# Attention with all PSUM banks, then 768 rows of one expert in fp16 parts, instead of fp32 blocks of four experts between

## The chip, the cores and the metric

One of the eight cores of a Trainium2 chip runs the whole kernel. The metric is the device time of one execution in microseconds, as the median of three runs. The core has five engines, each with an instruction queue of its own that is worked off strictly in order: TensorE (PE in the profile; its weight loads are PEld), VectorE (DVE), ScalarE (ACT), GpSimd (POOL), and SyncE (SP), which here only issues DMAs. TensorE writes to PSUM, which has eight banks of 128 x 512 fp32.

## The reference

Attention over 8 batches, 8 heads, 576 positions and 64 dims, causal with a window of 128 and a linear bias; then a mixture of experts over the 4608 tokens (512 wide), each of which goes to the best 2 of 8 experts (512 to 1024 to 512, with relu) by noisy logits.

```python
scores = scale * np.matmul(q, k.transpose(0, 1, 3, 2))
mask = (rel >= 0) & (rel < window)
scores = np.where(mask, scores + bias[None], -1000000000.0)
attn = softmax(scores)                      # in the reference: max, exp, sum + 1e-09
x = np.matmul(attn, v)                      # then tokens x heads*dims: 4608 x 512
noisy_logits = x @ w_gate + np.log1p(np.exp(x @ w_noise)) * noise
top2 = np.argpartition(-noisy_logits, 2, axis=1)[:, :2]      # top2_w: softmax of the two
for e in range(E):
    for k in range(2):
        mask = top2[:, k] == e
        h = np.maximum(x[mask] @ w1[e], 0.0)
        out[mask] += top2_w[mask, k, None] * (h @ w2[e])
```

## The kernel before

All instructions are written out by one Python program, and their order on each engine is set by a planner (class `Order`). Each piece of work is a strand, a generator that asks for an engine with an estimated duration and a rank; when an engine comes free in the planner's clock, it takes the ready piece of the least rank. Tables such as `STAGE`, `GATE`, `LATE`, `TOP`, `SPLIT` and `SIZES` are ranks and estimated durations, so every number in them moves instructions. On the chip the queues then keep that order, whatever the real durations are.

Attention has 96 units: 32 pairs of heads (`k`), each in three groups of query blocks (`GROUPS`). A unit goes through these steps: `scores` (TensorE, L482 and L475, into one of the pairs of banks in the ring `sb`), `top` (Vector: selects the window, L503 and L498, and adds the bias and takes the row's extreme, L508, from PSUM into `p` and `nm`), `soft` (ACT, exp with sum, L515), `trans` (TensorE, L522, into a bank of `tb`), `evac` (ACT or Vector, to `pT`, L262 or L266), `split` (GpSimd, two selects, L542 and L543), `weigh` (TensorE, L563, into a bank of `ob`), and a copy to `xu`. When four pairs have filled a group of a batch, `rows`, `row_major` and `gate` turn it to tokens (L663, L666), send it to DRAM (`xs`) and form the gate logits (L686, L697, L702, L707).

`route(b)` routes a batch: top 2 of the logits, counts by matmuls with a triangle (L754 to L758), places in expert lists (`base`, `line`), and one-hot matrices `hot` (L790, L796) whose product (L801) is the batch's contribution to the lists in DRAM (`slots`), which GpSimd adds by an indirect DMA (L874). In the kernel before, `route(b)` starts when `route(b - 1)` has been sent.

The FFN takes rows of an expert in blocks of up to 512. `tokens` gathers them by indirect DMA (GpSimd, L1068), `turn_tokens` transposes them (TensorE, L1100), `ups` does the first matrix (eight steps f of 128 hidden columns), `middle` applies relu, `downs` does the second, `result` scales and adds rows to `out` by an indirect DMA (GpSimd, L1254). There are two forms:
- first wave, fp32: 256 rows each of experts 0 to 3, of tokens of the first two batches (`CUTS = (2,)`), in the banks that attention leaves (`hb` is bank 5, results in banks of `tb` and `ob`). Matmuls L1117 and L1171.
- second wave, fp16 parts: each weight and each token is split in a high and a low fp16 part, and three products are summed (L1120, L1175, and L1180 where the result comes out turned). The split needs the largest magnitude of an expert's weights (`wam`, L1000 and L1021; `sized[e]`) and the scales of each token (`fit`, L1081 to L1085). It holds the other 960 rows of experts 0 to 3, and 1216 of experts 4 to 7.

What the two waves share is set in these lines:

```python
hb = bank[5]
sb, tb, ob, yb = Ring([bank[0:2]]), Ring([*bank[2:4], bank[7]]), Ring([bank[4], bank[6]]), Ring([])
BLOCKS = (((256, 512), (768, 448)), ((0, 512), (512, 384), (896, 320)))   # (start, rows): experts 0-3, 4-7
```

`banks` gives the score banks to the FFN when all of attention is done, and `second_wave` releases attention's SBUF tiles and makes ten sets of weight tiles when attention and all routing are done. The weights of expert e > 0 are sized once expert e - 1 has begun.

## Time and profile before

| | us |
|---|---|
| median of three runs | 1191.54 (1190.29 to 1195.24) |
| the profiled execution | 1194.33 |
| its span, first to last instruction | 1192.6 |
| TensorE busy in the span | 1125.3 |
| Vector busy | 716.3 |
| ACT busy | 484.9 |
| GpSimd busy | 311.4 |
| first fp32 FFN matmul | 143.1 |
| last of attention's weighing (L563) starts | 299.7 |
| first fp16 FFN matmul | 393.1 |

The page and the views give microseconds from the span's start. A row of a group has line, engine, operation, output and inputs, shape and count, then busy time, mean nanoseconds of one, and the idle time ahead of it with what ended it. Instructions of one engine overlap a little, so a mean times a count can be more than the busy time. The chain of work that ended last gives, from the end back, what each step waited for; its pieces are steps on the path and so show the real spacing of matmuls.

### The profile page before, as it was taken

The numbers are of one execution on the slowest core, as the hardware profiler recorded it, in microseconds if no ns is written. First come the engines' busy times: TensorE is split into PE (matmuls) and PEld (weight loads), VectorE is DVE, ScalarE is ACT, GpSimd is POOL, SyncE is SP. The second block draws the span as 40 slices with busy tenths as digits, with TensorE's granted clock in tenths as the row PEclk, the third lists the DMA queues.
The fourth block names the chain that finished last, engine by engine and source line by source line (L and its number), as shares of the span: only waits on it lengthen the run. The fifth ranks groups of instructions, "written<-read, shape, count | busy, mean of one in ns | idle before, by whom it ended". The sixth has DMA issues, their size and how long they took to land.

```text
span 1192.6 us, 20135 instructions
## 1 busy us (share of the span) xinstructions
PE 1125.3 (94%) x6940; PEld 648.1 (54%) x6940; DVE 716.3 (60%) x2528; ACT 484.9 (41%) x1309; POOL 311.4 (26%) x472
## 2 busy tenths in 40 slices
PE   7998899999998899999999999999989989999995
PEld 4665566666665445445445455456635654575552
DVE  6899988878766825645745745634743673372310
ACT  5776656655124314334334334233413532262311
POOL 2333433325123202311320330233203220232211
PEclk9999999999999999999999999999999999999998
DMA  9897555443658817626636644633823571342221
GB/s 324 271 340 255 155 179 161 152 145 86 186 148 252 246 42 203 173 58 186 173 74 186 177 84 162 177 63 64 244 83 64 123 231 37 63 117 45 36 27 24
DMA packets 133368, 173.32 MB, mean 145 GB/s; under 512 B 25232, under 2 KB 84880, under 8 KB 133264
## 3 DMA queue, kind: packets, MB, share of 16 engines
q1 hardware_dynamic: 115344, 131.68, 34.9%
q0 software_dynamic: 17920, 40.33, 17.8%
q8 instruction: 56, 0.92, 0.3%
q14 instruction: 48, 0.39, 0.1%
HBM read 130.57 MB, written 41.40 MB: 144 GB/s over the span
## 4 chain that ended last, share of the span: by engine, by line
PE 76%; DVE 10%; DMA 9%; issue 2%; POOL 1%; SPq 1%; ACT 1%; POOLq 0%; another core or an unknown queue 0%; DVEq 0%; ACTq 0%
PE bank L1120 26%; PE bank L1175 18%; PE bank L1180 9%; DMA mraw<-in_w_dram 5%; PE bank L563 4%; PE bank L1171 4%; PE bank L1117 3%; PE bank L482 3%; PE bank L1100 2%; DVE wam L1021 2%; PE bank L522 2%; DVE p L508 1%; PE bank L663 1%; DMA raw<-in_w_dram 1%; DMA w1a<-in_w_dram 1%
## 5 line engine op out<-in xcount | busy, mean ns | idle before, releaser
L1161 DVE SCALAR_TENSOR_TENSOR bhl<-bank,bhh 128x512 f16<-128x512 f32 (+3 forms) x160 | 97.3, 608 | 289.9 <-ACT bhh L1142 282.4
L1254 POOL DMA_INDIRECT out_dram<-yo,ix x72 | 113.0, 1570 | 573.6 <-ACT yo L262 468.5
L1120 PE MATMUL bank<-bxh,w1hb 128*128 128x512 f16 (+3 forms) x640 | 222.3, 347 | 0.0
L1120 PE MATMUL bank<-bxl,w1hb 128*128 128x512 f16 (+3 forms) x640 | 222.1, 347 | 0.0
L1120 PE MATMUL bank<-bxh,w1lb 128*128 128x512 f16 (+3 forms) x640 | 222.1, 347 | 0.0
L1142 ACT ACTIVATE bhh<-bank 128x512 f16<-128x512 f32 (+3 forms) x147 | 79.1, 538 | 349.6 <-PE bank L1120 348.0
L1120 PEld LDWEIGHTS <-w1hb 128*128 128x128 f16 x1280 | 124.3, 98 | 105.5 <-issue 2.2
L1175 PE MATMUL bank<-w2hb,bhl 128*128 128x512 f16 (+1 forms) x376 | 144.4, 384 | 1.2 <-DVE bhl L1161 1.2
L1175 PE MATMUL bank<-w2hb,bhh 128*128 128x512 f16 (+1 forms) x376 | 144.8, 385 | 0.5 <-ACT bhh L1142 0.5
L1175 PE MATMUL bank<-w2lb,bhh 128*128 128x512 f16 (+1 forms) x376 | 144.2, 383 | 0.0
L515 ACT ACTIVATE p<-p,nm 128x128 f32<-128x128 f32 x288 | 111.8, 393 | 19.2 <-DVE nm L508 18.6
L1175 PEld LDWEIGHTS <-bhh 128*128 128x128 f16 (+1 forms) x752 | 72.9, 99 | 80.8 <-issue 7.6
L1120 PEld LDWEIGHTS <-w1lb 128*128 128x128 f16 x640 | 62.6, 98 | 55.0
L482 PE MATMUL bank<-qk 64*128 64x256 f32 (+1 forms) x512 | 71.3, 391 | 18.7 <-DVE nm L508 13.1
L542 POOL TENSOR_SCALAR_AFFINE_SELECT pT<-pT 128x256 f32<-128x256 f32 (+2 forms) x96 | 43.9, 457 | 158.7 <-ACT pT L262 97.8
L1068 POOL DMA_INDIRECT xg<-xs_dram,ix x72 | 70.8, 984 | 42.9 <-issue 15.5
L563 PE MATMUL bank<-pT,vraw 128*64 128x128 f32 (+2 forms) x896 | 76.7, 303 | 5.0 <-POOL pT L543 3.7
L1021 DVE TENSOR_REDUCE wam<-mraw 128x1 f32<-128x1024 f32 x56 | 67.3, 1211 | 19.7 <-DMA mraw<-in_w_dram 17.7
L262 ACT ACTIVATE bxh<-bank 128x512 f16<-128x512 f32 (+1 forms) x71 | 40.6, 571 | 82.8 <-PE bank L1100 69.8
L1180 PE MATMUL bank<-bhl,w2hb 128*128 128x448 f16 (+1 forms) x224 | 73.8, 330 | 0.0
L1180 PE MATMUL bank<-bhh,w2lb 128*128 128x448 f16 (+1 forms) x224 | 73.8, 330 | 0.0
L1180 PE MATMUL bank<-bhh,w2hb 128*128 128x448 f16 (+1 forms) x224 | 73.8, 329 | 0.0
(208 smaller groups left out, 1818.6 us busy)
## 6 DMA issues: line engine op xcount, KB each, us to landing
raw<-in_w_dram SPq DMA_DIRECT2D x128, 256.0 KB
mraw<-in_w_dram SPq DMA_DIRECT2D x56, 512.0 KB
qk<-in_qk_dram SPq DMA_DIRECT2D x32, 608.0 KB
vraw<-in_v_dram SPq DMA_DIRECT2D x16, 640.0 KB
out_dram<-xg SPq DMA_DIRECT2D x10, 1024.0 KB
w1a<-in_w_dram SPq DMA_DIRECT2D x32, 256.0 KB
w2a<-in_w_dram SPq DMA_DIRECT2D x32, 256.0 KB
xs_dram<-x SPq DMA_DIRECT2D x32, 256.0 KB
```

What stands on the lines that cost most here:

```text
L482: nc.tensor.matmul(s[h][:, o:o + c], qk[half, i * 128:i * 128 + 128], qk[half, QW + k0:QW + k0 + c], start=True, stop=True)
L515: nc.scalar.activation(pv, pv, AF.Exp, bias=nm[:, z, h:h + 1], scale=-1.0, accum_out=den[:, z, 2 * g + h:2 * g + h + 1])
L563: nc.tensor.matmul(o[half, o0:o0 + c], t[:, kb, hh:hh + D], w, start=m == 0, stop=m == len(lst) - 1)
L1021: yield dve(1.13, rank, lambda: nc.vector.tensor_reduce(o, t, axis=AX.X, op=OP.max, apply_absolute_value=True))
L1068: yield pool(1.04, rank, lambda: nc.gpsimd.indirect_dma_start(out=xg[0:r], out_offset=None, in_=xs[0:blk.rows], in_offset=bass.IndirectOff ...
L1120: nc.tensor.matmul(t[:, 0:blk.n], wp[:, c], x[:, c, 0:blk.n], start=c == 0 and z == 0, stop=c == 3 and z == 2)
L1142: nc.scalar.activation(o, i, AF.Relu)
L1161: yield dve(0.07 + c * 0.00104, rank - MIDDLE, lambda: nc.vector.scalar_tensor_tensor(hl[:, 0:c], t[:, 0:c], 0.0, hh[:, 0:c], op0=OP.max, ...
L1171: nc.tensor.matmul(blk.y[j][0:r], blk.h[f][1][0][:, cs], w[1], start=f == 0, stop=f == 7)
L1175: nc.tensor.matmul(blk.y[j][0:r], h[:, cs], wp, start=f == 0 and m == 0, stop=f == 7 and m == 2)
L1180: nc.tensor.matmul(blk.y[c][:, 0:blk.n], wp[:, c * 128:c * 128 + 128], h[:, 0:blk.n], start=f == 0 and m == 0, stop=f == 7 and m == 2)
L1254: ins = nc.gpsimd.indirect_dma_start(out=out, out_offset=bass.IndirectOffsetOnAxis(ap=blk.ix[0:r, j:j + 1], axis=0), in_=t[0:r], in_offset ...
```

## The change

- Attention gets all eight banks: two pairs of score banks in place of one, two banks each for `tb` and `ob`. The counts of `route` go to a bank of `tb`. No FFN stands between.
- The fp32 wave is gone. `first` is now 768 rows of expert 0, of tokens of the first six batches (`CUT = 6`), as two blocks of 384 in fp16 parts; they stand behind attention and ahead of the other blocks, whose rows are now 448 of expert 0 and 1216 of each other expert. All blocks share one set of rings.
- Expert 0's weights are sized and split during attention into eight sets (`early_sizes`, for experts 0 and 1); the low parts of expert 0's weights are made by GpSimd in two instructions each, others by Vector as before. Ten more sets are added behind attention, as before, so there are 18.
- `route(b)` waits for batch b - 2 in place of b - 1, and has two sets of tiles; only the running counts (`based`) go from batch to batch. For all but the last batch GpSimd builds the one-hot matrices, in 20 instructions (ten of 128 x 80, ten of 128 x 64); Vector did so in eleven.
- The addition to `den` goes from Vector to GpSimd.
- The reads for the maxima of experts 2 to 7 are of 512 KB in one run, where a partition's 4 KB lay 16 KB apart.
- The planner's numbers are others throughout.

```diff
-CUTS = (2,)
-FIRST = (256,)
-NF = 4
+CUT, NF = 6, 1
+FIRST = ((0, 384), (384, 384))
...
-BLOCKS = (((256, 512), (768, 448)), ((0, 512), (512, 384), (896, 320)))
+BLOCKS = (((768, 448),), ((0, 512), (512, 384), (896, 320)))
...
-SIZES = (62.8, 977.3)
-EARLY = 1
+SIZES = (65.9, 147.7, 901.7)
+EARLY = 2
...
-    hb = bank[5]
-    rp = hb[:, 464:512].rearrange("p (i e) -> p i e", i=6)
-    hbr, own = Ring([hb]), Ring([hb])
-    sb, tb, ob, yb = Ring([bank[0:2]]), Ring([*bank[2:4], bank[7]]), Ring([bank[4], bank[6]]), Ring([])
+    sb, tb, ob = Ring([bank[0:2], bank[2:4]]), Ring([bank[7], bank[6]]), Ring([bank[4], bank[5]])
+    hbr, yb = Ring([]), Ring([])
...
-            nc.vector.tensor_scalar(den[0:nr, 0:nz], den[0:nr, 0:nz], 1e-9, None, op0=OP.add)
-            nc.vector.reciprocal(den[0:nr, 0:nz], den[0:nr, 0:nz])
+            nc.gpsimd.tensor_scalar(den[0:nr, 0:nz], den[0:nr, 0:nz], 1e-9, None, op0=OP.add)
+        yield pool(0.4 if nz == 1 else 0.2, rank, sums)
+        yield dve(0.2, rank, lambda: nc.vector.reciprocal(den[0:nr, 0:nz], den[0:nr, 0:nz]))
...
     def route(b):
         yield gates[b]
-        if b:
-            yield routed[b - 1]
+        if b > 1:
+            yield routed[b - 2]
+        y_, u, l, tp, idx, ef, oh, both_, d, gg, rk, oh2, lo_, si, gd, listed, *hot = route_sets[b % 2]
+        on, G = (dve, nc.vector) if b == B - 1 else (pool, nc.gpsimd)
...
-            V.tensor_tensor(hot[0], ef.rearrange("p i k -> p (i k)")[:, :, None].to_broadcast(shape),
-                            steps_[:, None, :].to_broadcast(shape), op=OP.is_equal)
+            if b == B - 1:
...
+            for i in range(NQ):
+                for k in range(2):
+                    G.tensor_scalar(hot[0][:, 2 * i + k], steps_, ef[:, i, k:k + 1], None, op0=OP.is_equal)
...
-                V.tensor_scalar(hot[1][:, 2 * i + k], steps_[:, 0:LINE], d[:, i, k:k + 1], numbers[:, i:i + 1],
+                G.tensor_scalar(hot[1][:, 2 * i + k], steps_[:, 0:LINE], d[:, i, k:k + 1], numbers[:, i:i + 1],
                                 op0=OP.is_equal, op1=OP.mult)
...
+        if b:
+            yield based[b - 1]
         yield from chain(taken, 0.0)
-        put(own, hb)
+        put(tb, a)
+        if b + 1 < B:
+            yield from chain(onward, 0.0)
+        mark(based[b])
...
+    def early_sizes():
+        yield biased[NP - 1]
+        for e in range(EARLY):
+            done = Event(16)
+            for f in range(8):
+                for z, (rg, src) in enumerate(((raw1, w1), (raw2, w2))):
+                    t = yield (rg, SIZES[e])
...
+            yield done
+            yield from powers_of_weights(e, SIZES[e])
...
-                    spawn(largest(rg, t, rank, wam[:, e % 2, z, q:q + 1], dram(src, e * DM * F + q * 1024, [[4096, 128], [1, 1024]]),
-                                  done))
+                    spawn(largest(rg, t, t, 1.13, rank, wam[:, e % 2, z, q:q + 1],
+                                  dram(src, e * DM * F + q * 131072, [[1024, 128], [1, 1024]]), done))
...
-        yield dve(0.6, rank, lambda: nc.vector.scalar_tensor_tensor(lo, t, sc, hi, op0=OP.mult, op1=OP.subtract))
+        def rest_of_weight():
+            nc.gpsimd.tensor_scalar(t, t, sc, None, op0=OP.mult)
+            nc.gpsimd.tensor_tensor(lo, t, hi, op=OP.subtract)
+        if e == 0:
+            yield pool(1.9, rank, rest_of_weight)
+        else:
+            yield dve(0.66, rank, lambda: nc.vector.scalar_tensor_tensor(lo, t, sc, hi, op0=OP.mult, op1=OP.subtract))
...
     def banks():
         yield attended
-        for t in sb.free.pop():
+        scores_ = [t for two in (sb.free.pop(), sb.free.pop()) for t in two]
+        for t in scores_[:3]:
             put(hbr, t)
-        t = yield (ob, 0)
-        put(yb, t)
+        put(yb, scores_[3])
+        for _ in range(2):
+            t = yield (ob, 0)
+            put(yb, t)
```

The order on the engines shows what moves. In the rows below, a name is followed by the number of its buffer (bank_66 to bank_73 are the eight banks, bank_66 and bank_67 the first pair), and x2 or x4 stands for so many instructions alike. First TensorE in the middle of attention, before: the scores of a unit (L482) take the only pair, bank_66 and bank_67, and between them and the next unit's scores stand transposes (L522), weighing (L563) and gate logits (L686).

```order
L482 MATMUL bank_66<-qk_79 128x128
L482 MATMUL bank_67<-qk_79 128x128
L482 MATMUL bank_66<-qk_79 128x256
L482 MATMUL bank_67<-qk_79 128x256
L697 MATMUL bank_69<-ident,gt_116 128x128 x2
L522 MATMUL bank_73<-ident,p_87 128x128
L563 MATMUL bank_72<-pT_94,vraw_82 64x256 x2
L563 MATMUL bank_72<-pT_94,vraw_82 64x128 x4
L686 MATMUL bank_73<-xu_98,wgn 32x256 x4
L482 MATMUL bank_66<-qk_79 128x256
L482 MATMUL bank_67<-qk_79 128x256
```

And now, at a like place (L479 and L472 are the scores, L560 the weighing):

```order
L472 MATMUL bank_68<-qk_81 128x192
L479 MATMUL bank_66<-qk_78 128x128
L479 MATMUL bank_67<-qk_78 128x128
L479 MATMUL bank_66<-qk_78 128x256
L479 MATMUL bank_67<-qk_78 128x256
L560 MATMUL bank_71<-pT_94,vraw_84 64x64 x4
L479 MATMUL bank_68<-qk_78 128x256
L479 MATMUL bank_69<-qk_78 128x256
```

The scores of three units stand nearly in a row, on two pairs of banks. Over the whole of attention TensorE has done the scores of 2.3 pairs of heads (as a mean) more than it has weighed, where it was 1.3.

Next GpSimd's queue in attention, before: selects alone (L542, L543), and a batch's lists going out (L874).

```order
L542 AFFINE_SELECT pT_95<-pT_95 128x128
L543 AFFINE_SELECT pT_95<-pT_95 128x128
L542 AFFINE_SELECT pT_96<-pT_96 128x2x128
L543 AFFINE_SELECT pT_96<-pT_96 128x2x128
L873 MEMSET pad 1x1
L874 DMA slots_dram<-listed,line_of_152 704x64
```

Now (L1045, L1046 the low part of a weight, L788, L793 the one-hot matrices, L632 the addition to den, L539, L540 the selects):

```order
L1045 TENSOR_SCALAR raw_123<-raw_123,wsc 128x512
L1046 TENSOR_TENSOR w2la_221<-raw_123,w2ha_220 128x512
L788 TENSOR_SCALAR hot_175<-steps,ef_164 128x80 x10
L632 TENSOR_SCALAR den_108<-den_108 128x16
L793 TENSOR_SCALAR hot_176<-steps,d_167,numbers 128x64 x2
L632 TENSOR_SCALAR den_109<-den_109 128x16
L793 TENSOR_SCALAR hot_176<-steps,d_167,numbers 128x64 x2
L539 AFFINE_SELECT pT_96<-pT_96 128x128
```

A unit's selects now stand behind eighteen other instructions.

Last, the end of attention on GpSimd now (L539 and L540 the selects of the last units, L1062 the gathers of the first rows of expert 0):

```order
L540 AFFINE_SELECT pT_94<-pT_94 128x2x128
L539 AFFINE_SELECT pT_95<-pT_95 128x4x128
L540 AFFINE_SELECT pT_95<-pT_95 128x4x128
L539 AFFINE_SELECT pT_96<-pT_96 128x128
L540 AFFINE_SELECT pT_96<-pT_96 128x128
L632 TENSOR_SCALAR den_103<-den_103 128x16
L632 TENSOR_SCALAR den_104<-den_104 128x16
L631 COPY den_105<-den_105 64x4
L632 TENSOR_SCALAR den_105<-den_105 64x8
L1062 DMA xg_124<-xs_dram,cl 128x520
L1062 DMA xg_125<-xs_dram,cl 128x520
L1062 DMA xg_126<-xs_dram,cl 128x520
```

The first rows are gathered behind the last select of attention (the lists of batch 5, which they need, go out five units earlier); before, the gathers of the first wave stood among the selects, halfway through attention.

More of the change, by code (lines that the diff above doesn't have):

```diff
@@ L321, in attention_moe @@
     tmp = const.tile([128, 2, E], F32, name="tmp")
-    line_of = [const.tile([E * SPAN, 1], I32, name=f"line_of{z}") for z in range(2)]
+    line_of = [const.tile([E * SPAN, 1], I32, name=f"line_of{z}") for z in range(3)]
     tops = const.tile([2, 1], F32, name="tops")
@@ L584, in unit @@
         s = yield (sb, r0)
-        yield pe((0.95, 1.2, 0.36)[gr], r0, lambda: scores(k, blocks, s), mode="rows" if nz == 2 else "full")
+        yield pe((0.77, 0.98, 0.325)[gr], r0, lambda: scores(k, blocks, s), mode="rows" if nz == 2 else "full")
         left[k] -= 1
@@ L939, in attention_moe @@
     back = keep.tile([128, E], F32, name="back")
-    seen = {(e, f): Event(2) for e in range(EARLY) for f in range(8)}
     sized = [Event() for _ in range(E)]
@@ L1042, in powers_of_weights @@
         mark(sized[e])
-    def all_powers():
-        for e in range(EARLY):
-            for f in range(8):
-                yield seen[e, f]
-            yield from powers_of_weights(e, ranks1[8 * e + 7] + SIZES[0])
     def scaled_weight(t, r, hi, lo, ev, rank, src, e, z, f):
@@ L1091, in turn_tokens @@
         yield order.now + 2.3
-        if blk in second:
-            yield from fit(blk, j, r, xg, rank)
+        yield from fit(blk, j, r, xg, rank)
         a = yield (tb, rank)
@@ L1115, in mm1 @@
         for c in cc:
-            if blk not in second:
-                nc.tensor.matmul(t[:, 0:blk.n], w[0][:, c], blk.xh[:, c, 0:blk.n], start=c == 0, stop=c == 3)
-                continue
             for z, (wp, x) in enumerate(((w[0], blk.xh), (w[0], blk.xl), (w[1], blk.xh))):
@@ L1169, in mm2 @@
         cs = slice(j * 128, j * 128 + r)
-        if blk not in second:
-            nc.tensor.matmul(blk.y[j][0:r], blk.h[f][1][0][:, cs], w[1], start=f == 0, stop=f == 7)
-            return
         hh, hl = blk.h[f][1]
@@ L1246, in result @@
         yield emptied
-        yield blk.back if blk in second else blk.weighed
+        yield blk.back
         t = yield (yor, rank)
@@ L1302, in second_wave @@
         for z in range(4):
-            put(fitr, more.tile([128, 3], F32, name=f"fit{z}"))
-        for z in range(4):
             put(ixr, more.tile([128, 4], I32, name=f"ix{z}"))
@@ L1308, in second_wave @@
         put(yb, t)
-        second.extend(Block(e, s0, c, NPAD, rings2) for e in range(E) for s0, c in BLOCKS[e >= NF])
-        for blk, after_ in zip(second, second[1:] + [None]):
-            blk.last = after_ is None or after_.e > blk.e
-            blk.flip = blk.last and after_ is not None
         for z in range(4):
-            put(ytr, more.tile([128, BLOCKS[0][1][1]], F32, name=f"yt{z}"))
-        steps = [(blk, f) for blk in second for f in range(8)]
-        ranks = [1000 + s for s in range(len(steps))]
-        spawn(ups(1, steps, ranks))
-        spawn(downs(1, steps, [r + 0.5 for r in ranks]))
+            put(ytr, more.tile([128, 448], F32, name=f"yt{z}"))
         spawn(second_tokens())
@@ L1403, in second_tokens @@
             yield from tokens(blk, 1000 + 8 * q - 7 if q else FFN1 - SOON)
+    second.extend(Block(e, s0, c, NPAD, rings) for e in range(E) for s0, c in BLOCKS[e >= NF])
+    for blk, after_ in zip(second, second[1:] + [None]):
+        blk.last = after_ is None or after_.e > blk.e
+        blk.flip = blk.last and after_ is not None
+    steps = [(blk, f) for blk in first + second for f in range(8)]
+    ranks = ranks1 + [1000 + s for s in range(8 * len(second))]
     nc.gpsimd.memset(ones, 1.0)
@@ L1416, in attention_moe @@
     order.at(1.9, lambda: order.dispatch("ACT"))
-    def last_weights():
-        yield named[0, NF - 1, 7]
-        yield from weights(1, lambda e, f: 1000 + step_of(e) + f - 4)
-    steps1 = [(blk, f) for blk in first for f in range(8)]
-    for strand in (loads(), masks(), all_values(), set_ups(), first_wave(), first_tokens(), banks(), second_wave(),
-                   weights(0, lambda e, f: ranks1[8 * e + f] - WEIGHTS), last_weights(), all_powers(),
-                   ups(0, steps1, ranks1), downs(0, steps1, [r + 0.3 for r in ranks1])):
+    for strand in (loads(), masks(), all_values(), set_ups(), first_tokens(), banks(), second_wave(), early_sizes(), weights(),
+                   ups([(*s, r) for s, r in zip(steps, ranks)]), downs([(*s, r + 0.4) for s, r in zip(steps, ranks)])):
         spawn(strand)
```

305 lines of the change are left out of this document (131 added, 174 removed).

## The prediction

> **What bounds the kernel now.** I read the page's busy line first, then a table by stage, then the softmax's progress in the same stages, then the waits inside attention.
>
> ```profile
> PE 1125.3 (94%) x6940; PEld 648.1 (54%) x6940; DVE 716.3 (60%) x2528; ACT 484.9 (41%) x1309; POOL 311.4 (26%) x472
> ```
> ```profile
> 0.00:30.00 30.00, 21.06 (x126) 13.89 (x126) 20.43 (x91) 17.66 (x68) 8.32 (x35) 1.00 1.01 324
> 30.00:143.00 113.00, 99.49 (x968) 68.62 (x969) 105.26 (x559) 74.67 (x325) 44.09 (x89) 1.00 0.80 267
> 143.00:290.00 147.00, 141.43 (x1192) 94.06 (x1191) 120.91 (x621) 85.71 (x371) 51.47 (x104) 1.00 0.48 144
> 290.00:323.00 33.00, 32.85 (x252) 20.92 (x251) 25.83 (x116) 8.41 (x31) 6.79 (x13) 1.00 0.52 153
> 323.00:393.00 70.00, 65.67 (x291) 43.53 (x290) 45.18 (x180) 24.23 (x50) 17.69 (x21) 0.98 0.74 209
> 393.00:480.00 87.00, 83.30 (x420) 41.32 (x418) 47.59 (x110) 30.32 (x52) 17.66 (x20) 1.00 0.55 149
> 480.00:1150.00 670.00, 652.18 (x3544) 351.58 (x3543) 347.70 (x855) 237.71 (x406) 155.98 (x180) 0.99 0.47 117
> ```
> Columns: stage, its length, busy us of PE, PEld, DVE, ACT, POOL, then granted clock, DMA share, GB/s. TensorE is the bound almost everywhere, but not in 30 to 143, where attention runs without FFN: there PE has 99.49/113 = 88% and Vector 105.26/113 = 93%. From 143, with fp32 FFN between, PE has 96% and Vector falls to 82%. From 393 the fp16 FFN holds PE at 96 to 97%.
>
> ```profile
> 0.00:30.00 30.00, 9.17 (x44) 1.00 1.01 324
> 30.00:143.00 113.00, 51.19 (x244) 1.00 0.80 267
> 143.00:290.00 147.00, 58.41 (x283) 1.00 0.48 144
> ```
> These are the softmax line's pieces on ACT (576 in all): 2.16 per us alone, 1.93 beside FFN. So alone attention is limited by Vector, and little faster than in company.
>
> ```profile
> PEld bank L482 <- DVE nm L508: 10.8, 17, 1.3
> PE bank L482 <- DVE nm L508: 6.7, 11, 1.0
> DVE bank L503 <- PE bank L482: 1.5, 3, 0.7
> ```
> In 30 to 143 TensorE's scores wait for Vector's top of the unit before (one pair of score banks), and Vector sometimes for the scores.
>
> **The change, step 1: the matmuls.**
>
> ```profile
> 341.75 1.73 PE bank L1117 x8
> 340.03 1.72 PE bank L1171 x4
> 426.83 2.59 PE bank L1175 x12
> 429.42 2.59 PE bank L1120 x12
> 1062.42 3.26 PE bank L1180 x24
> 412.95 0.44 PE bank L1100 x4
> ```
> From the chain: one fp32 step (256 rows, one f) is 1.73 + 1.72 = 3.45 us; 32 of them are 110.4 us, inside and just behind attention. An fp16 step of 512 rows is 2.59 + 2.59 = 5.18, so 10.12 ns a row (3.26 for 24 matmuls of 320 rows is the same rate). The 1024 rows cost 1024 x 8 x 10.12 ns = 82.9 us in fp16 parts: 27.5 us of PE work less, but all 82.9 now stand behind attention. Token tiles turned stay 80, but eight more lie in the fp16 part; three results fewer are turned back: (8 - 3) x 0.44 = 2.2 us.
>
> So with S the start of fp16 FFN (393 before), the span is 1192.6 - (393 - S) + 82.9 + 2.2 - idle saved later. It breaks even near S = 310. All hangs on S.
>
> **Step 2: Vector's work up to the last top.** By 290, where the tops end, Vector was busy 20.43 + 105.26 + 120.91 = 246.6 us.
>
> ```profile
> L796 DVE TENSOR_SCALAR hot<-steps,d,numbers 128x64 f16<-128x64 f16 x61 | 17.6, 346 | 0.0
> L790 DVE TENSOR_TENSOR hot<-ef,steps 128x800 f16<-128x800 f32 x7 | 7.2, 1033 | 0.0
> L266 DVE COPY pT<-bank 128x512 f32<-128x512 f32 x21 | 14.5, 689 | 5.7 <-PE bank L522 3.1 <-PE bank L475 2.3 <-issue 0.3
> L1000 DVE TENSOR_REDUCE wam<-w1a 128x1 f32<-128x512 f32 x8 | 5.4, 680 | 2.3 <-DMA w1a<-in_w_dram 2.3
> L635 DVE TENSOR_SCALAR den<-den 128x16 f32<-128x16 f32 x16 | 2.8, 177 | 0.0
> ```
> Off Vector: the hot matrices of five batches, 5 x (1.03 + 10 x 17.6/61) = 19.6; additions to den, about 5; evictions and scalings of the fp32 FFN, about 5 (from 290 us of the same list); some seven pT and seven xu copies that the order now gives ACT, about 8. Onto Vector: maxima of a second expert, 16 x 0.68 = 10.9; some dozen high parts of expert 0's weights, about 5.5; one more batch routed before the last top, about 8; small casts, 3. Sum -10, of which the overlap of neighbouring instructions takes a fifth: -8, so 239 us.
>
> GpSimd gets the hot matrices, den and 16 pairs of low parts.
>
> ```profile
> L542 POOL TENSOR_SCALAR_AFFINE_SELECT pT<-pT 128x512 f32<-128x512 f32 x32 | 21.5, 671 | 42.8 <-ACT pT L262 34.4 <-DVE pT L266 7.2 <-DVE d L827 1.0
> L542 POOL TENSOR_SCALAR_AFFINE_SELECT pT<-pT 128x128 f32<-128x128 f32 x32 | 9.4, 293 | 19.8 <-ACT pT L262 18.8 <-DVE pT L266 1.1
> L378 POOL IOTA steps<- 128x80 f16 x1 | 0.2, 209 | 0.0
> ```
> No tensor_scalar runs on POOL here. Nearest are the 128x80 iota (0.21) and the 128x128 select (0.29); the upper end is a 128x512 select (0.67). I take 0.25, the width being 64 to 80. 120 such by the last top are 30 us (25 to 80); the weight pairs 16 x (0.67 + about 1.0) = 27. To 290 the queue was busy 8.32 + 44.09 + 51.47 = 103.9 us by the table, and the same selects stay; with these 57 some 161 of 260 us, 62%. That is no bound by itself; but the queue is in order, the splits stand behind it, and TensorE's weighing behind the splits. Cover: scores now run 2.3 pairs ahead of the weighing in TensorE's order, against 1.3.
>
> ```profile
> L796 DVE TENSOR_SCALAR hot<-steps,d,numbers 128x64 f16<-128x64 f16 x20 | 4.4, 312 | 0.0
> ```
> This is L796 in 330 to 352, with GpSimd quiet: 0.22 us each, against 0.29 in attention. So Vector's instructions that touch only SBUF lose some 0.07 to GpSimd's neighbours. With GpSimd's share going from 103.9/290 = 36% to 62%, but the 80 longest of them gone, I add 3: 242 us. The Trainium skill (SBUF — State Buffer, § Who interferes with whom) says more: a GpSimd instruction and a Vector one that needs the shared port pair exclude each other for the whole instruction. The trace agrees in kind; by full blocking the last top would come some 30 us later, which is the fourth rival.
>
> With double score banks I take Vector at 96% (93% is the row's own value, 100% the other end): T = 30 + (242 - 20.4)/0.96 = 261 (252 to 268).
>
> ```profile
> L1117 PE MATMUL bank<-axh,w1a 128*128 128x256 f32 x119 | 33.7, 393 | 0.0
> L1171 PE MATMUL bank<-w2a,ahh 128*128 128x512 f32 x56 | 28.2, 608 | 0.0
> ```
> These are the FFN groups of 143 to 323. Their durations overlap, so I take the chain's spacing, 1.73/8 and 1.72/4: 119 x 0.216 + 56 x 0.43 = 50. TensorE's own attention work is then the four stages' 294.8 - 50 - 1 (token turns) = 244 us, of which about 236 lie before the last top: 90%. The row had 88%, so it fits, but with little room.
>
> **Step 3: from the last top to the first FFN matmul.** The gathers of the 768 rows stand on POOL behind the last select.
>
> ```profile
> 122.03 1.44 POOL L874 DMA_INDIRECT slots_dram<-listed,line_of  x1 [1.47 <-DVE bank L498]
> 127.81 1.29 SPq L910 DMA_DIRECT2D list<-slots_dram  x2
> 131.89 1.02 POOL L1068 DMA_INDIRECT xg<-xs_dram,cl  x1 [0.70 <-DVE cl L895]
> 143.10 0.60 PE L1117 MATMUL bank<-axh,w1a 128*128 128x256 f32 x2
> ```
> The old cut: scatter 122.03, gather 131.89, first matmul 143.10, that is 9.9 and 11.2 us. The scatter of batch 5 now stands five of 96 units (5 x 261/96 = 13.6 us) ahead of the last select, so the list is there; the gather comes at about T + 6 (softmax, transpose, eviction, split, then the clipped numbers on Vector). Behind it 11.2, plus the fit that first-wave tokens did not have: three tiles of about 1.3 on Vector and 0.7 on ACT, some 4. S = T + 21 = 282 (T + 12 if half is hidden, T + 30 if tokens queue). TensorE has only the last turns for these 20 us, some 8: it idles about 10.
>
> ```profile
> 321.18 0.25 PE bank L686 x8
> 359.22 1.00 POOL L1068 DMA_INDIRECT xg<-xs_dram,ix  x1 [6.05 <-PE bank L1171]
> ```
> The 448 remaining rows of expert 0 need the last two routings. Before, from the last gate logits (321) to the first gather (359) took 38 us; with 15 behind it that is 53, and the FFN of 768 rows covers 768 x 8 x 10.12 ns = 62: hidden.
>
> **Step 4: later idle.** 393 to 480 has 87 - 83.3 = 3.7 us idle, 480 to 1150 has 17.8.
>
> ```profile
> PE bank L459 <- DVE wmx L1029: 5.9, 2, 3.0
> DVE wam L1021 <- DMA mraw<-in_w_dram: 17.7, 14, 2.3
> ```
> It comes at the change of experts: Vector waits in order for maxima of the next expert's weights. One expert more is sized early (-3.7). Contiguous reads and 18 weight sets for 10 may take from 0 to 17.8 of the others; I take 2, since the reduce stays behind the load.
>
> **Sum:** 1192.6 - 111 + 82.9 + 2.2 - 6 = 1160.7. The profiled run was 1194.33, 1.7 above its span and 2.8 above the median 1191.54; so 1160.7 + 1.7 - 2.8 = 1160 as a median.
>
> **Rivals.**
> First, attention becomes TensorE's: both engines full (T = 252), half the transition hidden (S = 264), 15 us of later idle gone: 1192.6 - 129 + 85.1 - 15 - 1 = 1133. For it: double score banks. Against: 244 us of TensorE in 252.
> Second, the start of expert 0 is late: tokens queue behind routing on Vector, S = 300: 1192.6 - 93 + 85.1 - 4 - 1 = 1180. For it: gathers behind the last select. Against: the old cut's 11.2 us.
> Third, slower: TensorE stands, in order, before each batch's list matmuls until GpSimd has built that batch's 20 pieces. At 0.25 they take 5 us, at the 128x512 select's 0.67 13.4, some 8.4 more; six batches make 50 us, S = 332, 1192.6 - 61 + 85.1 - 4 - 1 = 1212. It decides from 5 us a batch (S = 312). Against: ops of 64 to 80 columns.
> Fourth, no change: if each added GpSimd instruction (120 hot, 32 for weights, 32 for den) held up Vector for half its length: 15 + 14 + 2 = 31 us, S = 313, 1193. Against: tops read PSUM, and only routing and weights would be hit.
>
> **Chances.** Likeliest, 1147 to 1174, 0.50; first rival 0.17; second, with all of 1174 to 1185, 0.14; fourth 0.09; third 0.10. About 0.5% (6 us) is what a measurement tells from no change. So faster 0.81, same 0.09, slower 0.10. The range that leaves no more than 2 in 10 out: 1135 to 1190; half of it is S, the rest later idle.
>
> **What would show it.** In the changed profile: the last top near 261 with Vector at 95% or more from 30 on; first fp16 matmul near 282 with about 10 us of idle TensorE ahead; softmax pieces at 2.3 to 2.5 per us; hot pieces on POOL near 0.25; no wait of TensorE over 5 us before the 448 rows; 5.18 us for a 512-row step as now. Wrong if Vector stays below 85% in attention, with TensorE waiting for splits or hot matrices, or if FFN starts after 310.

## The result, and the profile after

The change made the kernel slower: 1207.11 us (median of four runs, 1203.02 to 1208.70) against 1192.53 for the kernel before beside it (1190.29 to 1195.24), ratio 1.0116, 95% interval 1.0081 to 1.0151: a small loss, but clear of the spread. The forecast was 1160. The profiled run took 1203.02 with a span of 1201.1, which is 40.4 us more than the 1160.7 of the sum.

The same stages of the changed kernel (columns as before: window, length, busy us of PE, PEld, DVE, ACT, POOL, granted clock, DMA share, GB/s):

```profile
0.00:30.00 30.00, 23.50 (x183) 16.73 (x184) 22.95 (x128) 22.94 (x98) 10.78 (x41) 1.00 0.86 310
30.00:143.00 113.00, 98.00 (x931) 67.35 (x930) 95.97 (x490) 75.06 (x324) 80.91 (x147) 0.94 0.79 271
143.00:290.00 147.00, 125.83 (x1195) 85.00 (x1193) 120.85 (x642) 91.05 (x382) 117.41 (x224) 0.92 0.51 164
290.00:323.00 33.00, 23.20 (x158) 13.33 (x156) 24.52 (x123) 7.04 (x17) 7.49 (x12) 0.74 0.22 62
480.00:1150.00 670.00, 658.31 (x3776) 373.50 (x3775) 334.81 (x855) 230.36 (x395) 161.40 (x186) 0.99 0.44 106
```

Vector should have been at 96% from 30 on. It is at 95.97/113 = 85% and 120.85/147 = 82%. TensorE is no fuller (87 and 86%), and its granted clock, 1.00 in every attention stage before, is 0.94 and 0.92. The engine that has changed is POOL: 10.78 + 80.91 + 117.41 = 209.1 us up to 290, against 103.9 before and 161 in the prediction.

Cutting attention where routing begins, at 100 us, shows when that happened. First softmax's pieces (ACT busy, clock, DMA share, GB/s), then all engines in the same windows:

```profile
30.00:100.00 70.00, 34.30 (x166) 1.00 0.86 295
100.00:140.00 40.00, 13.21 (x64) 0.83 0.69 232
140.00:262.00 122.00, 48.11 (x232) 0.93 0.59 194
```
```profile
30.00:100.00 70.00, 65.77 (x659) 45.51 (x659) 65.42 (x333) 53.10 (x231) 39.14 (x78) 1.00 0.86 295
100.00:140.00 40.00, 29.23 (x242) 19.55 (x240) 27.69 (x143) 20.27 (x86) 38.93 (x67) 0.83 0.69 232
140.00:262.00 122.00, 105.08 (x1011) 71.27 (x1011) 105.41 (x565) 79.57 (x333) 97.69 (x180) 0.93 0.59 194
```

Up to 100 us attention runs as forecast: 166/70 = 2.37 pieces per us, TensorE and Vector both at 93 to 94%. From 100 to 140 it falls to 1.60, Vector to 69%, and POOL stands at 38.93/40 = 97%. What POOL runs there, from its groups by shape up to 300 us (count, busy us, mean ns of one, idle before):

```profile
L793 POOL TENSOR_SCALAR hot<-steps,d,numbers 128x64 f16<-128x64 f16 x60 | 34.5, 595 | 0.5
L788 POOL TENSOR_SCALAR hot<-steps,ef 128x80 f16<-128x80 f16 x60 | 27.8, 481 | 0.5 <-DVE ef L764 0.3
L1045 POOL TENSOR_SCALAR raw<-raw,wsc 128x512 f32<-128x512 f32 x16 | 25.5, 1592 | 4.4 <-DVE lo L761 2.8 <-DVE w1ha L263 1.1 <-DVE both L823 0.4
L1046 POOL TENSOR_TENSOR w1la<-raw,w1ha 128x512 f16<-128x512 f32 x8 | 9.4, 1170 | 0.7
```

In what follows the ten pieces of L788 (128x80) are a batch's line pieces, the ten of L793 (128x64) its place pieces. They take 0.48 and 0.60 us each, not 0.25, so a batch's twenty take 10.8 us; a low weight part takes 1.59 + 1.17 = 2.76, not 1.67. How that reaches TensorE is seen in the first batch routed (timeline of the changed kernel; start, us, engine, line, and in brackets how long the engine had been idle and for whom):

```profile
118.37 4.59 POOL L788 TENSOR_SCALAR hot<-steps,ef 128x80 f16<-128x80 f16 x10
...
122.95 2.24 POOL L793 TENSOR_SCALAR hot<-steps,d,numbers 128x64 f16<-128x64 f16 x4
123.58 0.21 PE L798 MATMUL bank<-hot,hot 128*80 128x64 f16 x1 [4.94 <-POOL hot L793]
...
124.46 0.22 DVE L803 COPY listed<-bank 80x64 f32<-80x64 f32 x1 [4.86 <-PE bank L798]
125.14 0.42 POOL L539 TENSOR_SCALAR_AFFINE_SELECT pT<-pT 128x256 f32<-128x256 f32 x1
```

TensorE stands before a list matmul for 4.94 us, Vector behind it for 4.86, and the next split (L539) comes only after ten line pieces and four place pieces. The ten line pieces are not this batch's: its own had run from 103.65, and eight of its place pieces by 118.4. They are the second batch's, which the order puts ahead of the first batch's last two place pieces; that can happen because `route(b)` no longer waits for batch b - 1. Over attention the waits are (us, times, longest), of PE and then of DVE, both from 100 to 290:

```profile
PE bank L798 <- POOL hot L793: 9.6, 7, 4.9
PE bank L560 <- POOL pT L540: 8.9, 7, 3.2
```
```profile
DVE den L635 <- POOL den L632: 7.4, 5, 2.6
DVE listed L805 <- PE bank L798: 7.3, 4, 3.1
DVE listed L803 <- PE bank L798: 4.9, 1, 4.9
```

All five wait for POOL, directly or by one step. The end of it, from the timeline: the last top, the first gather, the first FFN matmul.

```profile
282.76 0.29 DVE L505 CUSTOM_DVE_ANT_0 p<-bank,bias 128x128 f32<-128x128 f32 x1
290.68 1.09 POOL L1062 DMA_INDIRECT xg<-xs_dram,cl  x1 [1.78 <-DVE l L815]
307.99 0.52 PE L1107 MATMUL bank<-xh,w1ha 128*128 128x384 f16 x1
```

So T = 283 in place of 261 and S = 308 in place of 282. What lies behind S, after and before:

```profile
308.00:1150.00 842.00, 818.35 (x4618) 456.10 (x4617) 438.81 (x1167) 291.85 (x500) 210.88 (x251) 0.99 0.45 111
```
```profile
393.00:1142.00 749.00, 727.48 (x3917) 388.49 (x3915) 393.68 (x960) 265.75 (x453) 173.63 (x200) 0.99 0.48 121
```

TensorE has 90.9 us more work (85.1 were forecast) and 23.7 us idle in place of 21.5 (15.5 were forecast). Counted to the end, 893.1 us follow S; 878.7 were forecast.

### The profile page after: what moved, and what is told of

Its sections match the earlier page's. It is cut to its first block, busy times and chain, and to the rows that moved or that the text cites. A ratio compares the mean times of both kernels' runs of the same rounds, so it can differ in the third digit from the quotient of the medians.

```text
span 1201.1 us, 20775 instructions
## 1 busy us (share of the span) xinstructions
PE 1111.9 (93%) x7192; PEld 649.4 (54%) x7192; DVE 696.6 (58%) x2491; ACT 493.9 (41%) x1327; POOL 432.4 (36%) x676
## 4 chain that ended last, share of the span: by engine, by line
PE 60%; DMA 5%; DVE 5%; issue 1%; ACT 0%; POOL 0%; another core or an unknown queue 0%; POOLq 0%; DVEq 0%; ACTq 0%
PE bank L1107 28%; PE bank L1151 21%; PE bank L1156 8%; DMA mraw<-in_w_dram 4%; PE bank L1093 2%; DVE wam L1014 2%; DMA raw<-in_w_dram 1%; DVE xl L1100 0%; DMA xg<-xs_dram,ix 0%; PE bank L1209 0%; DVE hl L1142 0%; DMA xg<-xs_dram,cl 0%; DVE yo L263 0%; DVE fit L1079 0%; POOL out_dram L1228 0%
## 5 line engine op out<-in xcount | busy, mean ns | idle before, releaser
L1142 DVE SCALAR_TENSOR_TENSOR hl<-bank,hh 128x384 f16<-128x384 f32 (+3 forms) x192 | 110.8, 578 | 296.1 <-ACT hh L1127 295.7
L1151 PEld LDWEIGHTS <-hh 128*128 128x128 f16 (+1 forms) x928 | 89.4, 98 | 96.6 <-issue 5.8
L1107 PE MATMUL bank<-xh,w1hb 128*128 128x320 f16 (+2 forms) x384 | 129.9, 338 | 0.0
L1107 PE MATMUL bank<-xl,w1hb 128*128 128x320 f16 (+2 forms) x384 | 129.9, 338 | 0.0
L1107 PE MATMUL bank<-xh,w1lb 128*128 128x320 f16 (+2 forms) x384 | 129.8, 338 | 0.0
L1107 PE MATMUL bank<-xl,w1ha 128*128 128x384 f16 (+3 forms) x384 | 129.7, 338 | 0.0
L1107 PE MATMUL bank<-xh,w1ha 128*128 128x384 f16 (+3 forms) x384 | 129.7, 338 | 0.0
L1107 PE MATMUL bank<-xh,w1la 128*128 128x384 f16 (+3 forms) x384 | 129.7, 338 | 0.0
L1151 PE MATMUL bank<-w2ha,hl 128*128 128x512 f16 (+1 forms) x234 | 89.3, 382 | 1.2 <-DVE hl L1142 1.2
L1151 PE MATMUL bank<-w2ha,hh 128*128 128x512 f16 (+1 forms) x234 | 89.4, 382 | 0.0
L560 PE MATMUL bank<-pT,vraw 128*64 128x128 f32 (+2 forms) x896 | 76.4, 306 | 9.6 <-POOL pT L540 9.6
L1062 POOL DMA_INDIRECT xg<-xs_dram,ix x74 | 72.4, 979 | 34.1 <-issue 15.2
L479 PE MATMUL bank<-qk 64*128 64x256 f32 (+1 forms) x512 | 72.4, 404 | 12.8 <-DMA qk<-in_qk_dram 6.5
```

Of the source, the lines that this page charges most:

```text
L479: nc.tensor.matmul(s[h][:, o:o + c], qk[half, i * 128:i * 128 + 128], qk[half, QW + k0:QW + k0 + c], start=True, stop=True)
L560: nc.tensor.matmul(o[half, o0:o0 + c], t[:, kb, hh:hh + D], w, start=m == 0, stop=m == len(lst) - 1)
L1062: yield pool(1.04, rank, lambda: nc.gpsimd.indirect_dma_start(out=xg[0:r], out_offset=None, in_=xs[0:blk.rows], in_offset=bass.IndirectOff ...
L1107: nc.tensor.matmul(t[:, 0:blk.n], wp[:, c], x[:, c, 0:blk.n], start=c == 0 and z == 0, stop=c == 3 and z == 2)
L1142: yield dve(0.07 + c * 0.00104, rank - MIDDLE, lambda: nc.vector.scalar_tensor_tensor(hl[:, 0:c], t[:, 0:c], 0.0, hh[:, 0:c], op0=OP.max, ...
L1151: nc.tensor.matmul(blk.y[j][0:r], h[:, cs], wp, start=f == 0 and m == 0, stop=f == 7 and m == 2)
```

## The experiments

In real_prices and hot_on_vector_planned the planner orders everything anew, and before_hot_on_gpsimd has the order of the kernel before. In all other kernels the planner sees the same prices, so every engine's order is that of the changed kernel, save that the named instructions are issued on another engine or slot. Medians are of 4 to 12 runs. T is the last top and S the first fp16 FFN matmul in the profiled run. The kernels ran on several chips, so they are best compared by the ratios, each to the kernel before on the same chip.

| kernel | median us | ratio (95%) | T | S |
|---|---|---|---|---|
| the changed kernel | 1207.1 | 1.0116 (1.0081 to 1.0151) | 283 | 308.0 |
| hot_on_vector | 1188.8 | 0.9949 (0.9925 to 0.9972) | 270 | 295.3 |
| low_on_vector | 1203.1 | 1.0062 (1.0038 to 1.0087) | 278 | 302.6 |
| hot_low_on_vector | 1192.9 | 0.9969 (0.9951 to 0.9986) | 273 | 298.2 |
| real_prices | 1202.1 | 1.0036 (1.0010 to 1.0062) | 280 | 306.1 |
| half_hot | 1188.5 | 0.9961 (0.9942 to 0.9980) | 268 | 293.0 |
| other_half | 1192.0 | 0.9963 (0.9946 to 0.9979) | 271 | 295.8 |
| half_hot_block | 1195.6 | 1.0024 (0.9996 to 1.0051) | 278 | 303.4 |
| spread_line | 1210.7 | 1.0159 (1.0124 to 1.0193) | 291 | 315.3 |
| hot_on_scalar | 1211.0 | 1.0162 (1.0129 to 1.0196) | 284 | 308.5 |
| hot_on_vector_planned | 1199.3 | 1.0052 (1.0032 to 1.0073) | 289 | 296.0 |
| before_hot_on_gpsimd | 1238.0 | 1.0387 (1.0346 to 1.0429) | | |
| half_hot_warm | 1188.8 | 0.9960 (0.9942 to 0.9979) | 269 | 296.1 |
| half_hot_warm_free | 1188.0 | 0.9946 (0.9922 to 0.9969) | 269 | 294.1 |
| half_hot_warm_long | 1188.3 | 0.9931 (0.9918 to 0.9944) | 271 | 297.2 |

**Which of GpSimd's new work.** First the hot matrices, then the low parts, then both go back to Vector.

```diff
-        on, G = (dve, nc.vector) if b == B - 1 else (pool, nc.gpsimd)
+        on, G = dve if b == B - 1 else pool, nc.vector      # hot_on_vector; line pieces as one wide compare
```
```diff
-            nc.gpsimd.tensor_scalar(t, t, sc, None, op0=OP.mult)
-            nc.gpsimd.tensor_tensor(lo, t, hi, op=OP.subtract)
+            nc.vector.scalar_tensor_tensor(lo, t, sc, hi, op0=OP.mult, op1=OP.subtract)   # low_on_vector
```

> The hot matrices of batches 0 to 6 are built by Vector again (one wide compare and ten narrow ones a batch) at the very places where GpSimd had them; the order of TensorE and of all other work is that of the changed kernel, row for row. Theory A, GpSimd's queue holds attention up once routing begins (at 100 us): GpSimd loses some 62 us up to 283, Vector gains about 24, its idle time takes them; tops end near 270 in place of 283, FFN starts near 295, the time falls by 10 to 15 to about 1194, and TensorE's granted clock is near 1.0 from 100 to 260. Theory B, the two in-order queues of TensorE and Vector wait on each other whatever GpSimd does: Vector's 24 us come on top, tops end at 283 to 300, time 1207 to 1225.

> The 16 low weight parts of expert 0 are made by Vector (one instruction of 0.66 us each) in place of GpSimd's pairs of 1.59 and 1.17; TensorE's order unchanged. Theory A: GpSimd loses 44 us, Vector gains 10.6; tops end near 275, time about 1199. Theory B: tops end at 283 to 294, time 1207 to 1218.

> Both of these moves. GpSimd is then about as busy as before the change (some 100 us up to 283), Vector has 35 us more. Theory A: tops end between 262 and 270 with Vector at 97% or more, FFN starts near 290, time about 1188 to 1192. Theory B: tops end at 285 or later, time 1210 to 1240.

Theory A held, theory B fell: T and S come where A had them, and the time falls by 18 us (20 by the ratios) although Vector gets the work back. The windows of hot_on_vector:

```profile
100.00:140.00 40.00, 33.76 (x303) 22.95 (x300) 38.79 (x195) 24.08 (x103) 25.25 (x36) 0.83 0.76 248
140.00:262.00 122.00, 107.78 (x1031) 72.28 (x1029) 117.55 (x610) 80.52 (x334) 68.14 (x118) 0.94 0.60 195
```

Vector is now at 97 and 96%, as forecast for the change itself, POOL at 63 and 56%. One thing of A did not come: the clock is 0.83 and 0.94, as before the move. The low parts alone give 4 us (6 by the ratios) of the 8 expected, and the two intervals just overlap. Both moves together give no more than the first; Vector is at 97% in both windows by then.

**The load or the order?** The planner charged 4.2 us for a batch's hot pieces, which take 10.8.

```diff
-        yield on(0.98 if b == B - 1 else 2.2, rank, which_line)
+        yield on(0.98 if b == B - 1 else 4.8, rank, which_line)
-            yield on(0.4, rank, lambda: which_place(i))
+            yield on(0.6 if b == B - 1 else 1.2, rank, lambda: which_place(i))
-            yield pool(1.9, rank, rest_of_weight)
+            yield pool(2.75, rank, rest_of_weight)
```

> Only the planner's prices change: ten line pieces 4.8 us in place of 2.2, two place pieces 1.2 for 0.4, a low part 2.75 for 1.9, as measured; engines as in the changed kernel, the order planned anew. Theory A (the load on GpSimd itself): GpSimd still has the same 200 us, gain at most 5, time 1202 to 1210. Theory C (the order: the planner put bursts of cheap-looking pieces ahead of splits): the burst of ten pieces no longer stands before a split or a list matmul that is due, waits of TensorE for hot pieces under 3 us in all, tops end near 270, time about 1194.

1202.1, at theory A's lower end: an order that knows the prices wins 5 us (9.5 by the ratios) of the 47 missed. It does keep TensorE from standing before list matmuls, but TensorE's weighing still waits 9.1 us for splits from 100 to 290, against 8.9. The order counts too, though: hot_on_vector planned anew, with Vector's prices, is 10 us slower than in the inherited order.

> As hot_on_vector, but the planner knows that Vector builds them (0.98 us for the line, 0.6 for a pair of place pieces) and orders everything anew. If the engine's load decides, the time is that of hot_on_vector within 5 us, 1184 to 1194. If the order is what decides, tops end 5 or more earlier, time under 1183.

```diff
-        on, G = (dve, nc.vector) if b == B - 1 else (pool, nc.gpsimd)
+        on, G = dve, nc.vector                              # the planner is told 0.98, and 0.6 for a pair
```

Neither expectation. From 100 to 140 us it is worse than the changed kernel (36 softmax pieces for 64). POOL's timeline there, and PE's waits from 100 to 140:

```profile
116.76 2.42 POOL L1045 TENSOR_SCALAR raw<-raw,wsc 128x512 f32<-128x512 f32 x1 [6.48 <-ACT w1ha L261]
...
131.15 1.47 POOL L877 DMA_INDIRECT slots_dram<-listed,line_of  x1 [3.13 <-DMA slots_dram<-listed,line_of]
```
```profile
PE bank L560 <- POOL pT L540: 5.0, 2, 4.4
PE bank L746 <- DVE x L663: 4.3, 1, 4.3
```

POOL stands 6.48 us before a low weight part, works off three of them, and stands 3.13 before a scatter; no split lies between, and weighing waits 4.4 for the next. It is the same fault as the hot pieces', with other work.

**How much of the hot work is too much.** Two kernels leave half of it on GpSimd: the place pieces (half_hot, 5.8 us a batch) or the line pieces (other_half, 4.8).

```diff
-            if b == B - 1:
+            if True:                                        # half_hot: one wide compare on Vector, all batches
-                G.tensor_scalar(hot[1][:, 2 * i + k], ...
+                V.tensor_scalar(hot[1][:, 2 * i + k], ...   # other_half, alone
```

> Of each batch's twenty hot pieces only the ten for the line go back to Vector, as one wide compare of about 1.05 us; the ten for the place stay with GpSimd. TensorE's order unchanged. Load theory: GpSimd loses 6 x 4.8 = 29 of the 62 us up to the last top, so about half of the 18 us that moving all of them gave: tops end near 276, time 1195 to 1200. If what matters is the single longest burst of ten pieces ahead of a split, nearly all of it comes back: 1189 to 1193. If GpSimd were not the limit: 1207 or more.

> The mirror of half_hot: the ten place pieces of a batch go back to Vector (0.3 us each, at the slots where GpSimd had them), the ten line pieces stay on GpSimd as one block of 4.8 us. TensorE's order unchanged. Sum theory (what counts is a batch's GpSimd time against the 4.2 us that the order leaves for it): nearly nothing is lost, 1187 to 1194, less or equal to half_hot_block (5.8 in one block). Block theory (a block ahead of splits costs 1 to 2 us each time whatever the sum): 1195 to 1201.

Either half gives back what moving all gave, within the intervals: the loss is not proportional to the load. Two more kernels change only where in GpSimd's queue the same pieces lie. half_hot_block issues half_hot's ten place pieces in one block in the first slot; spread_line keeps all twenty on GpSimd, but deals the ten line pieces out over the five later slots.

```diff
-                return                                      # half_hot_block, on half_hot: in which_line's slot
+            for i in range(NQ if b < B - 1 else 0):
+                for k in range(2):
+                    G.tensor_scalar(hot[1][:, 2 * i + k], ...
```
```diff
-                    G.tensor_scalar(hot[0][:, 2 * i + k], ...   # spread_line, on the changed kernel
             for k in range(2):                              # in which_place(i)
+                if b < B - 1: G.tensor_scalar(hot[0][:, 2 * i + k], ...
                 G.tensor_scalar(hot[1][:, 2 * i + k], ...
```

> GpSimd has exactly the pieces of half_hot (ten place pieces a batch, the line compare on Vector), but issued as one block of ten (5.8 us) in the first slot, not as five pairs with room for splits between. TensorE's order unchanged. Burst theory: the loss returns, 1198 to 1207. Load theory: as half_hot, 1185 to 1192.

> All hot pieces stay on GpSimd, the same 62 us of them up to the last top; only the block of ten line pieces (4.8 us without a split between) is dealt out over the five later slots, two line and two place pieces (2.2 us) to a slot. TensorE's order unchanged. Burst theory (what counts is how long a due split or list matmul stands behind GpSimd work that is not due): nearly all of the 18 us comes back, tops end at 268 to 272, time 1187 to 1194. Load theory (62 us more on GpSimd, wherever): nothing comes back, 1203 to 1210.

With half the work the block costs 7 us, in the direction of the burst theory, though 1195.6 lies between the two ranges. TensorE's weighing waits for splits from 100 to 290 in half_hot, then in half_hot_block:

```profile
PE bank L560 <- POOL pT L540: 1.6, 4, 0.6
```
```profile
PE bank L560 <- POOL pT L540: 6.9, 5, 2.8
```

With all of the work on GpSimd, spreading gives nothing back, against the burst theory. Waits of spread_line from 100 to 290, PE and DVE:

```profile
PE bank L798 <- POOL hot L793: 19.7, 15, 5.6
PE bank L560 <- POOL pT L540: 6.8, 4, 6.0
```
```profile
DVE listed L805 <- PE bank L798: 24.0, 5, 5.7
```

The splits now come between (8.9 to 6.8), and the list matmuls wait for it: 9.6 to 19.7, and Vector behind them 24. So both are limits: a batch's pieces have some 4 to 6 us in this order. 4.8 fit even as one block, 5.8 fit if splits may pass, and 10.8 fit in none of the three layouts tried (as planned, spread, and planned with real prices). Why a block of 4.8 costs nothing and one of 5.8 costs 7 us is not shown further; Vector's share of the pieces differs too between those two kernels.

**One part alone, in the kernel before.** The same twenty pieces go to GpSimd, with nothing else changed.

```diff
-                V.tensor_scalar(hot[1][:, 2 * i + k], ...
+                (V if b == B - 1 else nc.gpsimd).tensor_scalar(hot[1][:, 2 * i + k], ...   # line pieces likewise
```

> The kernel before, with only this part of the change: the hot matrices of batches 0 to 6 built by GpSimd in twenty narrow pieces, everything else and the order as before. Load theory with cover: GpSimd is at 36% there, TensorE has fp32 FFN steps to run, batches are routed one after another, so little shows: 1190 to 1200. Rival: a burst of some 10 us ahead of splits and the list matmuls costs its 2 to 3 us a batch wherever it stands: 1205 to 1215.

Both expectations were far too small: 45 us, 6.4 for each of seven batches. POOL's groups up to 400 us, then PE's and DVE's waits from 30 to 393:

```profile
L801 POOL TENSOR_SCALAR hot<-steps,d,numbers 128x64 f16<-128x64 f16 x70 | 40.6, 671 | 0.0
L796 POOL TENSOR_SCALAR hot<-steps,ef 128x80 f16<-128x80 f16 x70 | 32.8, 550 | 24.9 <-DVE ef L772 24.9
```
```profile
PE bank L563 <- POOL pT L543: 22.0, 9, 7.2
PE bank L806 <- POOL hot L801: 9.3, 15, 4.5
```
```profile
DVE listed L813 <- PE bank L806: 20.1, 3, 15.0
```

PE's waits for splits were 2.9 us in the kernel before, in the same window. POOL, at 132.45/290 = 46% up to 290 here, and a second stream of FFN work on TensorE were no cover: the FFN matmuls stand in the same in-order queue, behind the one that waits.

**ScalarE instead.** The place pieces become two activations each, the line pieces one wide compare on Vector.

```diff
-                G.tensor_scalar(hot[1][:, 2 * i + k], steps_[:, 0:LINE], d[:, i, k:k + 1], numbers[:, i:i + 1], ...
+                t = hot[1][:, 2 * i + k]; nc.scalar.activation(t, steps_[:, 0:LINE], AF.Abs, bias=d[:, i, k:k + 1], scale=-1.0)
+                nc.scalar.activation(t, t, AF.Relu, bias=numbers[:, i:i + 1], scale=less[:, i:i + 1])
```

> The line pieces are one wide compare on Vector, the place pieces two activations each on ScalarE (absolute difference, then a clipped ramp times the token's number), all in the same slots; TensorE's order unchanged. GpSimd builds nothing hot before the last batch. Theory that Vector, at 97%, is what ends attention once GpSimd is relieved: Vector loses some 18 us against hot_on_vector, ScalarE (66% busy there) gains 20 x 0.21 = 4.2 us a batch; tops end at 262 to 266 in place of 270, time 1180 to 1185. Rival: softmax and evictions stand behind ScalarE's bursts as splits stood behind GpSimd's; tops end at 270 or later, time 1188 to 1200.

The rival held, and worse than it said, since the price was wrong again. ScalarE's groups of 100 to 290:

```profile
L794 ACT ACTIVATE hot<-hot,numbers,less 128x64 f16<-128x64 f16 x60 | 26.4, 439 | 2.0
L793 ACT ACTIVATE hot<-steps,d 128x64 f16<-128x64 f16 x60 | 20.0, 334 | 0.0
```

0.33 + 0.44 in place of 0.42 for a piece: 7.7 us a batch ahead of softmax and evictions, and T is that of the changed kernel.

**The clock behind the last top.** Between T and S TensorE of half_hot idles for 4.9 us in one piece, and its clock falls to 0.5. half_hot_warm puts fillers (matmuls whose result nobody uses) before the first token turn.

```diff
         def turn():
+            for _ in range(36 if blk is first[0] and j == 0 else 0):
+                nc.tensor.matmul(a[:, 0:128], ones, before, start=True, stop=True)
```

half_hot_warm_free writes `bank[0]` in place of `a`; half_hot_warm_long does so with 80 fillers.

> half_hot with 36 bf16 matmuls of 128 columns (0.06 to 0.11 us each) ahead of the first token turn, where TensorE stood idle for 4.9 us at a granted clock of 0.5; they compute nothing that is used. If the clock falls because of TensorE's idle time, the token turns and the first nine FFN matmuls (0.32 us each there, 0.16 later) run at full clock: FFN starts 1 to 2 us earlier and the whole is 2 to 4 us shorter than half_hot, about 1185. Rival: the clock is granted by something else (power, other engines), the row stays near 0.5, and the fillers cost 0 to 2 us: 1188 to 1191.

> As half_hot_warm, but the 36 filler matmuls write a score bank that has been free since the last top, so that they need not wait for Vector and run in the 4.9 us gap itself. If the clock follows TensorE's own activity, it is 1.0 when the token turns begin, eight turns take 1.04 us in place of 1.94, the first FFN matmuls are spaced 0.16, FFN starts about 1 us earlier and has no slow stretch: 2 to 4 us shorter than half_hot, about 1185. Rival: a filled gap takes as long as the gap, and nothing is won: 1188 to 1190.

> half_hot_warm_free with 80 fillers in place of 36: 4.8 us at full clock, as long as the gap. If the clock follows TensorE's activity, token turns take 1.04 for eight and the first FFN matmuls are spaced 0.16; FFN's first 12 matmuls and the turns save 2 to 3 us against half_hot: about 1186. Rival: no change, 1188 to 1190, because what TensorE wins there it waits for later.

TensorE's timeline in half_hot, half_hot_warm and half_hot_warm_free (fillers are L1092, token turns L1093 or L1094):

```profile
287.71 1.94 PE L1093 MATMUL bank<-ident,xg 128*128 128x128 f32 x8 [4.94 <-ACT xg L261]
```
```profile
288.41 3.59 PE L1092 MATMUL bank<-before,ones 128*128 128x128 bf16 x36 [4.66 <-DVE x L663]
291.83 1.04 PE L1094 MATMUL bank<-ident,xg 128*128 128x128 f32 x8
```
```profile
283.71 2.17 PE L1092 MATMUL bank<-before,ones 128*128 128x128 bf16 x36
288.81 1.94 PE L1094 MATMUL bank<-ident,xg 128*128 128x128 f32 x8 [2.93 <-ACT xg L261]
```

Right behind fillers eight turns take 1.04 us, otherwise 1.94: the clock follows TensorE's own activity. But nothing was won. The first fillers waited for a bank and came after the gap; the second ended 2.93 us early, and that idle time was enough for the clock to fall again; the third (80) met a clock that had already fallen, took 6.97 us and overran the gap. The intervals of all four overlap (ratios 0.9961, 0.9960, 0.9946, 0.9931); by the middle values this stretch is worth at most some 4 us, and no gain is shown.

**A version that beats both kernels** is half_hot (or hot_on_vector, equal within the intervals): 0.9961 of the kernel before (0.9942 to 0.9980), about 0.985 of the changed one. It is still 28 us above the forecast.

## Why the prediction was wrong

By the sum, 40.4 us are missing: S came 26 us late, idle time after it was 8.1 us more than forecast, TensorE's work 5.8 more, the tail 0.5. With half the hot pieces moved, S is 293: the pieces account for 15 of those 26 us, and for 18 of the 47 in the medians. Of the rest, the steps below say what the traces show; no run took it apart.

- **Step 1** held as far as it went. A 512-row second half still takes 2 x 2.59 us, by the chain of waits of the changed kernel:

```profile
458.26 5.18 PE bank L1151 x24
```

  That is two steps' second halves, 24 matmuls. The mis-sized term is what else lies behind S: 5.8 us more TensorE work than the 85.1. Part of it is the clock, 0.84 over the first 15 us and 0.94 over the next 27 (by estimate 2.4 + 1.3 us more for the same work); the rest, the last turns and list matmuls that now run there, was not tested apart. So it breaks even at 1192.6 - 893.1 = 299.5, not 310.
- **Step 2 is the step that failed**, in its second half. Vector's work was right (242 us forecast, 235.8 measured up to 283). GpSimd's was not: 57 us added were forecast, 105 came (209.1 - 103.9), and they were taken to cost attention no wait, covered by scores that run 2.3 pairs ahead, so that even their own upper bound (80 us for the hot pieces alone) did not enter T. They did make waits: 9.6 us of TensorE before list matmuls and 8.9 before weighing, and T came at 283 for 261. The piece was put at 0.25 us, "the width being 64 to 80", between bounds that held the true 0.48 and 0.60; the weight pair at 1.67 against 2.76. And "62%. That is no bound by itself" was the wrong question: in before_hot_on_gpsimd 46% was no bound either, and cost 45 us. With the hot pieces halved, T is 268, at the end of the range given for it (252 to 268). The clock is a rival for what is left: from 30 to 290 TensorE ran at half clock for 37.5 us in the changed kernel and 30.6 in half_hot, against none before, and no run kept it whole there.
- **Step 3**: S - T is 25 (21 forecast, 12 to 30) in the changed kernel and in half_hot alike; the gather comes at T + 7.6 (forecast T + 6), the other 2 us lie between gather and matmul, where the turns ran at half clock, and were not measured apart.
- **Step 4** came in its cause but not in its sum: idle is 23.7 us in place of 15.5. TensorE's 5.9 us of waiting for the next expert's maxima are gone, but its waits before token turns are 16.7 us (before: 11.9), and list matmuls wait behind S as well. Two rows of the changed kernel's waits from 308 to 1150:

```profile
PE bank L1093 <- issue: 10.1, 5, 2.4
PE bank L798 <- POOL hot L793: 2.9, 8, 0.4
```

- **The rivals.** The third is what happened: TensorE stands, in order, before the list matmuls until GpSimd has built the pieces, with the splits behind the same pieces. Its limit of 5 us a batch is near what the runs show (4.8 loses nothing, 5.8 nothing or 7 us by its layout, 10.8 loses in all three layouts). Its price was too high for the changed kernel, 8.4 us a batch against about 3 (18 us over six batches); why so little of a batch's 5.8 us of excess shows in the time was not tested. It had a chance of 0.10, on the ground "ops of 64 to 80 columns"; its own row, the 0.67 us select, was nearer to the truth than the 0.25 that was taken. The fourth is real, but small (its page sentence and its price do not agree: 31 us is half blocking by the prediction's rows, full blocking would be some 60): matched instruction by instruction, Vector's work up to 290 took some 8 us less in low_on_vector, nearly all of it in instructions that touch no PSUM, and some 2 less in hot_on_vector, so it is mostly the low weight parts that slow Vector. One such instruction, in the changed kernel and in low_on_vector:

```profile
L765 DVE CAST d<-si 128x10 f32<-128x10 int32 x6 | 2.3, 381 | 0.2
```
```profile
L765 DVE CAST d<-si 128x10 f32<-128x10 int32 x6 | 1.0, 174 | 0.2
```

The signs named in advance did tell: Vector at 85%, TensorE waiting for splits and hot pieces; S = 308 fell just short of the 310 named.

## What to carry to other kernels

An operation that moves to another engine has no price until a row of that engine shows it: between bounds of 0.21 and 0.67, take the end that hurts, or measure the piece first. An in-order engine at 46% is not free: ask what is due behind each new block in its queue, and who stands in order before the result; all twenty pieces cost 18 us in one kernel and 45 in another, ten of them 7 us or nothing, by how long they take against the time that the order leaves for them. And to tell load from order, move the work between engines with the planned order held fixed; planning anew alone moved the time by 10 us.
